# Scaled keys in eight tiles without a copy, weight maxima held to the end, and the staging of weights partly in x2T

## The chip, the cores and the metric

One core of one Trainium2 chip runs the whole program. The metric is device time in microseconds (us), the median of several runs; less is better.

## What is computed

The reference is a recurrent attention over 768 steps for 4 batches of 8 heads with a 40x40 state, followed by two dense layers on its 3072 rows of 320 values:

```
for t in range(S):
    y[:, :, t] = einsum('bhd,bhde->bhe', rt, state)
    Sa = einsum('bhde,bhe->bhd', state, at)
    state = state * wt[:, :, None, :] - outer(Sa, bt) + outer(vt, kt)
x = y as (3072, 320)
h = x @ w_in;  x = (h * cos(h)) @ w_out
h = x @ w_in2; out = (h * clip(h + 3, 0, 6) / 6) @ w_out2
```

The weights arrive as 64-bit floats.

## The kernel before

The 768 steps are cut into 12 chunks of 64. A unit n is one chunk of one batch, so there are 48. For a unit, `pA` loads r, k, a, b into `raw` and the running decay into `pip`; `pB` multiplies the two and splits the scaled keys into a high and a low half in `KBs` (L834 to L837) and the scaled queries likewise in `ARs`. `pT` transposes both by DMA to `KBT` and `ART`, and `pC` multiplies them on TensorE (tile `p`). `iB` inverts a triangular matrix for the four units of a chunk in 31 short steps on VectorE (tiles `tmp`, `Tt`, `Lt`). `cU`, `cA`, `cG` and `cF` compute the unit's output and the new state (tiles `u`, `FS`, `gm`, `GF`, `xy`, `S8a`, in PSUM mostly `t`). `cF` multiplies the keys in their natural layout once more. For that, `pB` copies the first 80 of every 128 columns of `KBs`, of which there are two tiles, into one of eight tiles `E` (L842, L843).

When the four units of a chunk are done, `mA` and `mB` run the first dense layer on its 256 rows (input `x1T`), and later the second (input `x2T`, which `mT` fills by DMA transposes). `mA` makes a PSUM tile `h`, ScalarE and VectorE make `s` from it and split it into two halves `ghl`, and `mB` adds the product with the weights up in `acc`. A layer of a chunk has 8 such groups. Below, a chunk's first multiplication means the first VectorE row that writes `s` from `h` in the first layer.

The weights come in 44 tiles of 128x512 values (22 for each layer). `ld_w` loads one to a staging place, `prep_w` turns it into a 32-bit value in a second staging place and splits it into two f16 halves in `win` and `wout`. The staging place is a piece of `wout` that is not filled yet or, for 16 tiles, `wstat` (`stage`, L735 to L748). `wmax` takes the largest absolute value of each finished tile on VectorE (a TENSOR_REDUCE into `acc` of the accumulators); the flags at the end of the program read it, and nothing before. A flag that fails starts a general path, which these data do not take.

The order of the instructions of each engine is not the order of the source. `Plan` records every operation with an estimated cost and its dependencies, goes forward and backward through a model of the engines `PASSES` times, and issues in the order of the last pass. An operation on `nc.either` goes to VectorE or GpSimd, or, for a copy, to VectorE or ScalarE, as the model finds it. So nearly every instruction carries the line of `emit` (L452, copies on ScalarE L448). All loads and transposes are issued by SyncE (SP).

Of the kernel before, what the change touches and what calls it, by code (L numbers as in the profile page):

```python
# [26 lines left out]
NT = B * S  # L27
HD = H * D
GRP = 4
NG = NC // GRP  # L30
SC = 256.0
ISC = 1.0 / 256.0
# [14 lines left out]

HALVES = ((0, 0), (1, 0))
SHARE = 20
SLACK, AHEAD, MARGIN = [0, 0, 0, 0, 0], [100, 100, 200, 0], [20, 20, 20, 0]  # L50
LAND = 1950
PASSES = 46
RING = {"raw": 2560, "KBT": 2048, "LN": 2048, "v": 1280, "uh": 640, "FT": 2048, "gm": 2048, "pd": 2560, "xy": 1280,
        "wst": 2048, "wx": 1024, "s": 2048, "xs2": 1536, "ghl": 2048, "E": 1280, "ART": 2048, "NT": 1152}


class Rings:
# [22 lines left out]
ALTS = {"ANY": ("DVE", "POOL"), "CPY": ("DVE", "ACT")}  # L80
T_SHAPE = 96.0
FULL = (128, 128)
POOL_GAIN = -0.03
OFFSET = 110
LAT = {"PE": 190, "DVE": 125, "ACT": 140, "POOL": 70}

# [1 line left out]
class Plan:  # L88
# [68 lines left out]
    def rec(self, attr, eng, name, a, kw):  # L157
# [25 lines left out]
        elif eng == "PE":  # L183
            m = _free(ins[0])
            c = max(n / 2.4 + 2.5, 25.0 if m == 128 else 32.0)
            if ins[0].dtype == F32:
                c = max(2 * (5 + 0.835 * m), 4 * n / 2.4)
            shape = tuple(32 if x <= 32 else 64 if x <= 64 else 128 for x in (ins[0].shape[0], _free(ins[0])))
        elif eng in ("DVE", "ANY"):
            c = 70 + n * 1.042  # L190
            es = max(mybir.dt.size(x.dtype) for x in outs + ins)
            if name == "tensor_copy":
                c = 70 + n * (0.26 if es == 2 else 0.52)
            elif name == "tensor_tensor" and n > 512 and any(len(x.ap) > 2 and abs(x.ap[-1][0]) > 4 for x in ins):
                c = 70 + n * 1.906
            elif name == "tensor_scalar":
                c = 70 + n * 0.52
            elif name == "reciprocal":
                c = 70 + n * 6.3
            elif name == "tensor_tensor_scan":  # L200
                c = 70 + n * 2.08
            if any(_free(x) == 1 for x in ins):
                c += 60
        elif eng == "ACT":
            c = 95 + n * 0.833
            if "accum_out" in kw:
                c += 93
            elif "bias" in kw:
                c += 50
            elif ins[0].tensor._space == PSUM:  # L210
                c -= 42
        rate = 2.56 if any(abs(x.ap[-1][0]) > 4 for x in ins) else 2.1 if all(mybir.dt.size(x.dtype) == 4 for x in outs + ins) else 1.88
        cp = 36 + n * 0.83 if name == "memset" else 150 + n * (rate if name == "tensor_tensor" else 3.4)
        if eng == "POOL":
            c = cp
        elif eng == "ANY" and name == "tensor_copy":
            eng, cp = "CPY", 95 + n * 0.833
        merge = eng == "PE" and self.ops and self.ops[-1]["eng"] == "PE" and self.ops[-1]["grp"] == (self.group, outs[0].tensor.name)
        if merge:
            i -= 1  # L220
# [121 lines left out]
    def forward(self, pr, pred, users):  # L342
# [41 lines left out]
        def arrive(u):  # L384
            e = ops[u]["eng"]
            ready_t[u] += SLACK[engs.index(e)] if e in engs else 0
            heapq.heappush(evs, (ready_t[u], 0, u))
            if e in engs[:4]:
                soon[engs.index(e)].add(u)
# [106 lines left out]
def kernel(  # L496
# [24 lines left out]
    p1 = Rings(big, 1)  # L521
    p2 = Rings(big, 2)
    p3 = Rings(big, 3)
    pE = Rings(big, 8)
    pA_ = Rings(big, 8)
    pN = Rings(big, 6)
    dr = pool("dr", 1, space=DRAM)
# [20 lines left out]
        COL[nm] = (ncol, ncol + k)  # L548
        ncol += k
    acc = fl.tile([128, ncol], F32, name="acc")  # L550
    KBss = [big.tile([128, H, 128], F16, name=f"KBs{i}") for i in range(2)]
    ARss = [big.tile([128, H, 128], F16, name=f"ARs{i}") for i in range(2)]
    pip0 = big.tile([128, H, 2, D], F32, name="pip0")
    TTp = big.tile([128, NH * C + 64], F16, name="TT")
# [169 lines left out]


    wflat = [t.rearrange("p x k f -> p x (k f)") for t in wout]
    wstat = big.tile([128, 1536], F32, name="wstat")
    junk = wstat[:, 1376:1536].bitcast(BF16)
    WST = {}

    def stage(m, kind, i):
# [4 lines left out]
        else:  # L736
            r, x = ((4, 8), (14, 18), (-1, 0), (4, 8), (14, 18), (-1, 0), (6, 18), (-1, 0), (-1, 0), (-1, 0))[i]
        if r < 0:
            return wstat[:, 0:1024], wstat[:, 1024:1536]
        w = wflat[m].rearrange("p x f -> p (x f)").bitcast(F32)  # L740
        return w[:, 256 * r:256 * r + 1024], w[:, 256 * x:256 * x + 512]

# [79 lines left out]
        ldq.dma_start(out=pip[0:64].rearrange("p h x e -> p h (x e)"), in_=dec(n).rearrange("h t x e -> t h (x e)"))  # L822
        st_raw[n] = (raw, pip)

    E_t = {}
    ART_t = {}
    KBT_t = {}

    def pB(n):
# [1 line left out]
        nc.either.tensor_copy(out=pip[64:128, :, 1], in_=pip[0:64, :, 1])  # L831
        rf = raw.rearrange("p h x e -> p (h x e)")
        nc.either.tensor_tensor(out=rf, in0=rf, in1=pip.rearrange("p h x e -> p (h x e)"), op=ALU.mult)
        kb, ar = KBss[n % 2], ARss[n % 2]  # L834
        kv = kb[:, :, 0:120].rearrange("p h (x e) -> p h x e", e=D)
        nc.either.tensor_copy(out=kv[:, :, 0::2, :], in_=bc2(raw[:, :, 1]))
        dp("kb", E_KB).tensor_tensor(out=kb[:, :, 40:80], in0=raw[:, :, 1], in1=kb[:, :, 0:40], op=ALU.subtract)  # L837
# [1 line left out]
        nc.either.tensor_copy(out=av, in_=bc2(raw[:, :, 0]))  # L839
        dp("ar", E_AR).tensor_tensor(out=ar[:, :, 80:120], in0=raw[:, :, 0], in1=ar[:, :, 0:40], op=ALU.subtract)  # L840
        square(rf, 0, 128, 640, "raw", n, rf)
        E_t[n] = pE.tile([128, H, 2 * D], F16, tag="E", name="E")  # L842
        nc.either.tensor_copy(out=E_t[n], in_=kb[:, :, 0:2 * D])  # L843
        later(0.7, pT, n)

    def pT(n):
        KBT_t[n] = p1.tile([128, H, 128], F16, tag="KBT", name="KBT")
        ART_t[n] = pA_.tile([128, H, 128], F16, tag="ART", name="ART")
        tq.dma_start_transpose(out=KBT_t[n], in_=KBss[n % 2].rearrange("p h e -> p (h e)"))
        tq.dma_start_transpose(out=ART_t[n], in_=ARss[n % 2].rearrange("p h e -> p (h e)"))  # L850

    NT_t = {}
# [188 lines left out]

    def cF(n):
        c, b = divmod(n, B)
        pd, kb, art = PD_t.pop(n), E_t.pop(n), ART_t.pop(n)
        gh, gl = ([t[:, h * (C + D):h * (C + D) + 128] for h in range(H)] for t in GFt)
        f = ps_t.tile([128, 512], F32, tag="t", name="gf")
        fv = f[:, 0:HD].rearrange("p (h e) -> p h e", h=H)
# [457 lines left out]
```

## Time and profile before

| | before |
|---|---|
| median of 3 runs | 1179.76 us (1177.58 to 1183.35) |
| the profiled execution | 1175.69 us |
| its span, first to last instruction | 1173.9 us |
| TensorE busy | 891.6 us, 76% |
| VectorE busy | 1009.4 us, 86% |
| ScalarE busy | 824.4 us, 70% |
| GpSimd busy | 200.8 us, 17% |
| mean granted TensorE clock | 0.966 |

Busy times are the time in which an engine has at least one instruction under way. In the trace PE is TensorE, PEld its weight loads, DVE VectorE, ACT ScalarE, POOL GpSimd, SP the queue of SyncE. Rows give a group of equal instructions as "out<-in", their number, the busy time and the mean time of one in ns, and then the idle time of the engine before them with what ended it.

### The profile page before, as it was taken

What the parts mean: (1) busy time and instruction counts of PE and PEld (TensorE: products, weight loads), DVE (VectorE), ACT (ScalarE), POOL (GpSimd) and SP (SyncE); (2) the same over time, 40 slices, a digit from 0 to 9 for tenths busy, and PEclk for the clock granted to TensorE, in tenths of its full rate; (3) what the DMA queues carried; (4) which work ended last, traced back from release to release, by engine and by line L of the source; (5) the groups of instructions that cost most, each with busy time, mean ns of one, the idle gap of its engine ahead of it and who ended that gap; (6) DMA issues with size and microseconds to landing.
All of it is one profiled execution on the core that took longest, in us unless ns stands there. A gap on an engine that the chain in (4) does not pass through costs nothing. (4 is left out here: it accounts for less than half of the span.)

```text
span 1173.9 us, 29549 instructions
## 1 busy us (share of the span) xinstructions
PE 891.6 (76%) x11378; PEld 727.0 (62%) x11378; DVE 1009.4 (86%) x2282; ACT 824.4 (70%) x1701; POOL 200.8 (17%) x225
## 2 busy tenths in 40 slices
PE   0010042265997999999999998999999999999994
PEld 0000031264775887787788777777778878788873
DVE  7799999979998999799998998988989879676552
ACT  5667688778988778688697876867758747563341
POOL 3340223433433102011020110300201000000000
PEclk9999999987998999899999999998999999999997
DMA  6988879978887677977778976797775773521010
GB/s 210 243 193 202 225 180 227 195 166 166 190 171 139 122 134 133 169 143 132 142 118 173 167 132 127 134 157 139 129 142 103 112 136 62 98 55 32 1 26 15
DMA packets 474361, 162.63 MB, mean 139 GB/s; under 512 B 446790, under 2 KB 456050, under 8 KB 473827
## 3 DMA queue, kind: packets, MB, share of 16 engines
q1 hardware_dynamic: 473922, 159.99, 68.8%
q8 instruction: 91, 1.49, 0.6%
q10 hardware_dynamic: 288, 0.67, 0.2%
q14 instruction: 60, 0.48, 0.1%
HBM read 80.09 MB, written 25.61 MB: 90 GB/s over the span
## 5 line engine op out<-in xcount | busy, mean ns | idle before, releaser
L452 PE MATMUL acc<-wout,ghl 128*128 128x320 f16 x2304 | 361.0, 304 | 11.7 <-DVE xs L452 6.8
L452 PEld LDWEIGHTS <-win 128*128 128x128 f16 x3328 | 309.6, 101 | 55.4 <-issue 14.8
L452 PEld LDWEIGHTS <-ghl 128*128 128x128 f16 x2304 | 218.3, 99 | 92.5 <-issue 7.7
L452 ACT ACTIVATE s<-h,cvec 128x512 f32<-128x512 f32 x192 | 130.5, 680 | 120.5 <-PE h L452 70.7
L452 PE MATMUL h<-x1T,win 128*128 128x256 f16 (+1 forms) x1664 | 194.1, 276 | 10.8 <-DVE s L452 10.4
L452 PE MATMUL h<-x2T,win 128*128 128x256 f16 (+1 forms) x1664 | 184.4, 266 | 2.5 <-DVE s L452 2.5
L452 DVE TENSOR_TENSOR ghl<-s,ghl 128x512 f16<-128x512 f32 x185 | 128.2, 693 | 5.0 <-ACT ghl L448 2.6
L452 PE MATMUL p<-ART,KBT 120*128 120x64 f16 x384 | 21.9, 206 | 143.7 <-DMA ART<-ARs 90.9
L452 PEld LDWEIGHTS <-KBT 120*128 120x128 f16 x384 | 18.5, 106 | 147.6 <-DMA KBT<-KBs 110.4
L452 DVE TENSOR_TENSOR tmp<-Tt,Lt 128x126 f32<-128x126 f32 (+22 forms) x372 | 103.3, 278 | 7.7 <-DMA Lt<-Ls 4.1
L452 DVE TENSOR_TENSOR Tt<-Tt,tmp 128x126 f32<-128x126 f32 (+22 forms) x372 | 105.2, 283 | 3.9
L452 DVE SCALAR_TENSOR_TENSOR s<-h,s 128x512 f32<-128x512 f32 x96 | 65.6, 686 | 39.1 <-ACT s L452 38.3
L448 ACT ACTIVATE ghl<-s 128x512 f16<-128x512 f32 x121 | 75.4, 625 | 26.2 <-DVE s L452 21.7
L452 DVE SCALAR_TENSOR_TENSOR s<-s,h 128x512 f32<-128x512 f32 x96 | 65.1, 680 | 23.6 <-ACT s L452 23.4
L452 POOL TENSOR_TENSOR wout<-wout 128x512 int32<-128x512 int32 (+2 forms) x30 | 47.9, 1600 | 102.6 <-ACT wout L452 46.0
L452 PE MATMUL t<-E,GF 128*128 128x40 f16 x1152 | 45.4, 183 | 23.0 <-DVE GF L452 18.1
L452 PEld LDWEIGHTS <-GF 128*128 128x128 f16 x1152 | 38.3, 98 | 30.5 <-DVE GF L452 18.8
L452 PE MATMUL t<-FS,NT 128*128 128x40 f16 x768 | 36.6, 182 | 20.4 <-DVE FS L452 13.6
L452 PEld LDWEIGHTS <-ART 120*64 120x64 f16 (+1 forms) x704 | 43.1, 105 | 14.3 <-issue 10.6
L452 PE MATMUL q<-Lt,Tt 32*32 32x32 f32 x768 | 31.6, 199 | 23.4 <-DMA Lt<-Tm 22.5
L452 ACT ACTIVATE wout<-wout 128x512 f32<-128x512 f32 (+3 forms) x56 | 37.0, 662 | 15.6 <-DMA wout<-in_moe_w_in_dram 11.3
L452 POOL TENSOR_TENSOR wstat<-wstat 128x512 int32<-128x512 int32 (+1 forms) x16 | 30.4, 1898 | 102.5 <-ACT wstat L452 80.4
(163 smaller groups left out, 1744.7 us busy)
## 6 DMA issues: line engine op xcount, KB each, us to landing
raw<-in_arbk_dram SPq DMA_DIRECT2D x46, 320.0 KB
v<-in_vv_dram SPq DMA_DIRECT2D x96, 80.0 KB
pip<-Dec SPq DMA_DIRECT2D x46, 160.0 KB
wout<-in_moe_w_in_dram SPq DMA_DIRECT2D x12, 512.0 KB
Ls<-LN SPq DMA_DIRECT2D x48, 128.0 KB
Lt<-Ls SPq DMA_DIRECT2D x48, 128.0 KB
TT<-Thl SPq DMA_DIRECT2D x12, 512.0 KB
wstat<-in_moe_w_out_dram SPq DMA_DIRECT2D x10, 512.0 KB
```

What stands on the lines that cost most here:

```text
L448: self.nc.scalar.activation(func=AF.Copy, **kw)
L452: getattr(getattr(self.nc, attr), name)(*a, **kw)
```

## The change

`KBs` has eight tiles instead of two, `cF` reads them directly, and the tiles `E` and their 48 copies are gone. The operations of `wmax` are held in the planner's model until 900000 of its units. `wstat` has 1024 columns instead of 1536; the second staging place of the 16 tiles that are staged there is now a part of `x2T`, and the scratch output `junk` lies in the last 160 columns of what is left. The planner's numbers are others: its slack, look-ahead and margins, its number of passes, the gain from which it gives GpSimd an operation, and the cost of a cast of a strided output. Six more small memsets on GpSimd clear the ends of the new tiles.

```diff
+NKB = 8
-SLACK, AHEAD, MARGIN = [0, 0, 0, 0, 0], [100, 100, 200, 0], [20, 20, 20, 0]
+SLACK, AHEAD, MARGIN = [0, 49, 4, 0, 67], [50, 50, 0, 0], [0, 100, 50, 0]
-PASSES = 46
+HELD, HOLD = ("wmax",), 900000
+PASSES = 29
-POOL_GAIN = -0.03
+POOL_GAIN = 0.17
...
+        turn = name == "tensor_copy" and n > 512 and abs(outs[0].ap[-1][0]) > 4
+        if turn:
+            c = 70 + n * 1.906
...
-            eng, cp = "CPY", 95 + n * 0.833
+            eng, cp = "CPY", 70 + n * 1.906 if turn else 95 + n * 0.833
...
             ready_t[u] += SLACK[engs.index(e)] if e in engs else 0
+            if ops[u]["grp"][0][0] in HELD:
+                ready_t[u] = max(ready_t[u], HOLD)
...
-    KBss = [big.tile([128, H, 128], F16, name=f"KBs{i}") for i in range(2)]
+    KBss = [big.tile([128, H, 128], F16, name=f"KBs{i}") for i in range(NKB)]
...
-    wstat = big.tile([128, 1536], F32, name="wstat")
-    junk = wstat[:, 1376:1536].bitcast(BF16)
+    wstat = big.tile([128, 1024], F32, name="wstat")
+    junk = wstat[:, 864:1024].bitcast(BF16)
...
-            return wstat[:, 0:1024], wstat[:, 1024:1536]
+            return wstat, x2T.rearrange("p a b -> p (a b)").bitcast(F32)[:, 0:512]
...
-        kb, ar = KBss[n % 2], ARss[n % 2]
+        kb, ar = KBss[n % NKB], ARss[n % 2]
...
-        E_t[n] = pE.tile([128, H, 2 * D], F16, tag="E", name="E")
-        nc.either.tensor_copy(out=E_t[n], in_=kb[:, :, 0:2 * D])
...
-        tq.dma_start_transpose(out=KBT_t[n], in_=KBss[n % 2].rearrange("p h e -> p (h e)"))
+        tq.dma_start_transpose(out=KBT_t[n], in_=KBss[n % NKB].rearrange("p h e -> p (h e)"))
...
-        pd, kb, art = PD_t.pop(n), E_t.pop(n), ART_t.pop(n)
+        pd, kb, art = PD_t.pop(n), KBss[n % NKB], ART_t.pop(n)
```

How the order moves is seen at three places. The first is VectorE near the start of the program, while the first weights are split (`win_68` is the first layer's, `wout_70` its still empty second matrix that serves as staging, `FS` the first unit's values). Before:

```order
L452 SCALAR_TENSOR_TENSOR FS_82<-v_136,FS_82 128x8x40
L452 TENSOR_REDUCE acc<-win_68 128x1
L452 TENSOR_TENSOR win_68<-wout_70,win_68 128x512
L452 CAST win_68<-wstat 128x512
L452 TENSOR_REDUCE acc<-win_68 128x1
L452 TENSOR_TENSOR win_68<-wstat,win_68 128x512
L452 TENSOR_REDUCE acc<-win_68 128x1
```

and now:

```order
L460 TENSOR_TENSOR win_68<-wout_70,win_68 128x512
L460 SCALAR_TENSOR_TENSOR FS_88<-v_134,FS_88 128x8x40
L460 CAST win_68<-wout_70 64x512
L460 TENSOR_TENSOR win_68<-wout_70,win_68 64x512
L460 TENSOR_SCALAR wout_70<-wout_70 128x512
L460 SCALAR_TENSOR_TENSOR wout_70<-wout_70 128x512
L460 TENSOR_TENSOR win_68<-x2T,win_68 128x512
```

The maxima are gone from here; up to the first chunk's first multiplication VectorE has 441 instructions before and 403 now, with 28 maxima before and none now.

The second is VectorE in the last sixth of the program, where the first layer of the eleventh chunk runs (`s_145`, `s_146`) beside the last chunk's attention. Before:

```order
L452 SCALAR_TENSOR_TENSOR s_147<-h_145,s_147 128x512
L452 CAST ghl_150<-s_147 128x512
L452 TENSOR_TENSOR ghl_150<-s_147,ghl_150 128x512
L452 SCALAR_TENSOR_TENSOR s_148<-h_146,s_148 128x512
L452 CAST ghl_151<-s_148 128x512
L452 TENSOR_TENSOR ghl_151<-s_148,ghl_151 128x512
L452 SCALAR_TENSOR_TENSOR s_147<-h_145,s_147 128x512
```

and now:

```order
L460 SCALAR_TENSOR_TENSOR s_145<-h_143,s_145 128x512
L460 TENSOR_REDUCE acc<-wout_70 128x1 x7
L460 SCALAR_TENSOR_TENSOR s_145<-h_143,s_145 128x512
L460 TENSOR_REDUCE acc<-wout_70 128x1
L460 SCALAR_TENSOR_TENSOR s_146<-h_144,s_146 128x512
L460 TENSOR_REDUCE acc<-wout_70 128x1
L460 TENSOR_REDUCE acc<-win_69 128x1 x2
```

All 44 maxima now stand between the last multiplication of the tenth chunk's first layer and the first one of the last chunk's, 8 of them ahead of the eleventh chunk's first multiplication, and the subtractions into `ghl` that stood there go to GpSimd (7 in the program before, 17 now).

The third is SP, where the first chunk's `x2T` is filled (`xs`) for the second layer and the last weights of that layer are loaded to `wstat`. Before:

```order
L452 DMA_TRANSPOSE x2T<-xs_153 128x6x128
L452 DMA_TRANSPOSE FT_141<-FS_82 128x8x128
L452 DMA raw_116<-in_arbk_dram 128x640
L452 DMA_TRANSPOSE ST_87<-Tt 128x16x48
L452 DMA_TRANSPOSE KBT_125<-KBs_76 128x8x128
L452 DMA Srep_89<-Tt 40x16x40 x3
L452 DMA Tt<-Ls_104 32x32x32
L452 DMA_TRANSPOSE FT_141<-FS_83 128x8x128
L452 DMA wstat<-in_moe_w_out_dram 128x1024
L452 DMA pip_80<-Dec_99 64x8x80
L452 DMA_TRANSPOSE x2T<-xs_154 128x6x128
```

and now:

```order
L460 DMA wstat<-in_moe_w_out_dram 128x1024
L460 DMA_TRANSPOSE ST_93<-Tt 128x16x48
L460 DMA Srep_95<-Tt 40x16x40 x2
L460 DMA_TRANSPOSE FT_139<-FS_88 128x8x128
L460 DMA Srep_95<-Tt 40x16x40
L460 DMA Tt<-Ls_110 32x32x32
L460 DMA_TRANSPOSE x2T<-xs_151 128x6x128
L460 DMA_TRANSPOSE FT_139<-FS_89 128x8x128
L460 DMA v_134<-in_vv_dram 64x320 x2
L460 DMA_TRANSPOSE x2T<-xs_152 128x6x128
```

Before, two loads to `wstat` follow the first transpose into `x2T` (one stands here, one seven rows later); now every load to `wstat` precedes it.

## Rows read from the trace of the kernel before

**Rows 1.** The page's busy times: us, share of the span, instructions.

```profile
PE 891.6 (76%) x11378; PEld 727.0 (62%) x11378; DVE 1009.4 (86%) x2282; ACT 824.4 (70%) x1701; POOL 200.8 (17%) x225
```

**Rows 2.** Busy time of each engine in five stretches; columns as the first line says.

```profile
core 0: us, PE busy (x) PEld busy (x) DVE busy (x) ACT busy (x) POOL busy (x), PEclk, DMA share, GB/s
0.00:241.60 241.60, 38.17 (x688) 33.45 (x688) 219.25 (x423) 172.99 (x332) 69.73 (x78) 1.00 0.87 207
241.60:398.50 156.90, 122.04 (x1681) 100.34 (x1682) 144.50 (x316) 133.84 (x285) 58.81 (x50) 0.87 0.79 162
398.50:1002.00 603.50, 577.99 (x7394) 469.67 (x7392) 550.45 (x1349) 449.14 (x943) 72.28 (x98) 0.98 0.75 134
1002.00:1151.50 149.50, 147.50 (x1578) 119.70 (x1576) 91.08 (x184) 66.00 (x140) 0.00 (x0) 1.00 0.20 38
```

**Rows 3.** The same view for the whole start and for the stretch 960 to 1036.

```profile
0.00:398.50 398.50, 160.22 (x2368) 133.80 (x2369) 363.75 (x738) 306.82 (x617) 128.54 (x127) 0.95 0.84 190
960.00:1036.00 76.00, 73.47 (x940) 60.22 (x937) 61.44 (x161) 46.55 (x101) 2.59 (x3) 1.00 0.42 72
```

**Rows 4.** What writes the accumulators on VectorE: number, ns min/median/max, first and last start.

```profile
L452 DVE TENSOR_REDUCE acc<-win x24: 664/674/686, 31.4 to 295.9; 128x1 f32<-128x512 f16 x16, 64x1 f32<-64x512 f16 x8
...
L452 DVE TENSOR_REDUCE acc<-wout x20: 666/673/686, 129.4 to 391.7; 128x1 f32<-128x512 f16 x20
```

**Rows 5.** Groups by cost: the copies to E.

```profile
L448 ACT ACTIVATE E<-KBs 128x640 f16<-128x640 f16 x46 | 33.4, 727 | 0.8 <-PE t L452 0.4
...
L452 DVE COPY E<-KBs 128x640 f16<-128x640 f16 x2 | 0.7, 325 | 0.0
```

**Rows 6.** Groups on VectorE by form, of the kinds whose number changes most.

```profile
L452 DVE TENSOR_TENSOR ghl<-s,ghl 128x512 f16<-128x512 f32 x185 | 128.2, 693 | 5.0 <-ACT ghl L448 2.6
...
L452 DVE CAST ghl<-s 128x512 f16<-128x512 f32 x71 | 30.8, 433 | 6.4 <-PE acc L452 4.2 <-DVE s L452 0.5
...
L452 DVE TENSOR_TENSOR KBs<-raw,KBs 128x320 f16<-128x320 f32 x39 | 20.0, 512 | 1.3 <-ACT KBs L448 1.1
L452 DVE TENSOR_TENSOR ARs<-raw,ARs 128x320 f16<-128x320 f32 x37 | 18.5, 500 | 0.3 <-ACT ARs L448 0.2
...
L452 DVE CAST KBs<-raw 128x640 f16<-128x640 f32 x10 | 6.9, 690 | 0.1
...
L452 DVE COPY GF<-FS 128x320 f16<-128x320 f16 x28 | 6.6, 234 | 0.1
...
L452 DVE TENSOR_TENSOR wout<-wout 128x512 f16<-128x512 f32 x8 | 5.4, 680 | 0.0
...
L452 DVE CAST Tt<-S8a 40x640 f16<-40x640 f32 x6 | 2.9, 490 | 2.2 <-DMA Srep<-Tt 2.1
```

**Rows 7.** Waits on VectorE: us in total, times, longest.

```profile
DVE s L452 <- ACT s L452: 61.6, 51, 4.1
```

**Rows 8.** What touches KBT: the transposes, ns min/median/max.

```profile
L452 SPq DMA_TRANSPOSE KBT<-KBs x48: 1231/1272/2387, 49.2 to 945.6; - x48
```

**Rows 9.** VectorE in order of time near 28 us: start, duration.

```profile
27.98 1.51 DVE L452 TENSOR_SCALAR wout<-wout 64x512 int32<-64x512 int32 x1
...
31.42 0.69 DVE L452 TENSOR_REDUCE acc<-win 128x1 f32<-128x512 f16 x1 [0.81 <-ACT win L448]
```

**Rows 10.** GpSimd in order of time in the same stretch.

```profile
27.53 1.68 POOL L452 TENSOR_TENSOR wout<-wout 128x512 int32<-128x512 int32 x1 [18.08 <-DVE wstat L452]
30.40 1.36 POOL L452 TENSOR_TENSOR wstat<-wstat 128x512 int32<-128x512 int32 x1 [1.19 <-ACT wstat L452]
```

**Rows 11.** SP in order of time: the two transposes that fill x2T first.

```profile
330.41 1.26 SPq L452 DMA_TRANSPOSE x2T<-xs  x1
...
344.68 1.29 SPq L452 DMA_TRANSPOSE x2T<-xs  x1
```

**Rows 12.** TensorE in order of time: the second layer's first matmuls.

```profile
351.26 1.95 PE L452 MATMUL h<-x2T,win 128*128 128x128 f16 x32
```

**Rows 13.** VectorE in order of time: the last read of wstat by the weights.

```profile
385.46 1.35 DVE L452 TENSOR_TENSOR wout<-wstat,wout 128x512 f16<-128x512 f32 x1
```

More of the change, by code (lines that the diff above doesn't have):

```diff
@@ L49 @@
 SHARE = 20
-SLACK, AHEAD, MARGIN = [0, 0, 0, 0, 0], [100, 100, 200, 0], [20, 20, 20, 0]
+SLACK, AHEAD, MARGIN = [0, 49, 4, 0, 67], [50, 50, 0, 0], [0, 100, 50, 0]
 LAND = 1950
-PASSES = 46
+HELD, HOLD = ("wmax",), 900000
+PASSES = 29
 RING = {"raw": 2560, "KBT": 2048, "LN": 2048, "v": 1280, "uh": 640, "FT": 2048, "gm": 2048, "pd": 2560, "xy": 1280,
-        "wst": 2048, "wx": 1024, "s": 2048, "xs2": 1536, "ghl": 2048, "E": 1280, "ART": 2048, "NT": 1152}
+        "wst": 2048, "wx": 1024, "s": 2048, "xs2": 1536, "ghl": 2048, "ART": 2048, "NT": 1152}
 class Rings:
@@ L523 @@
     p3 = Rings(big, 3)
-    pE = Rings(big, 8)
     pA_ = Rings(big, 8)
@@ L823, in pA @@
         st_raw[n] = (raw, pip)
-    E_t = {}
     ART_t = {}
```

## The prediction

> **What bounds the kernel now.** I read the page's busy times first, then the busy times by stretch, because an average over this program hides that its stages have different limits. TensorE is busy for 891.6 of 1173.9 us [rows 1]. Cut at the first dense matmul (241.6 us), at the first layer of the third chunk (398.5) and at that of the eleventh (1002), the stretches show two limits [rows 2]. Up to 241.6 us TensorE works 38.17 us while VectorE is busy for 219.25, or 91%; up to 398.5 us VectorE is still at 144.50 of 156.90, or 92%. After that TensorE has little idle time left: 25.5 us of 603.5 (603.50 less 577.99), then 2.0 us of 149.5. VectorE is close behind it in the long middle, 550.45 of 603.50, and free in the last stretch, 91.08 of 149.50.
>
> So the end is TensorE's work plus its idle time, and 238 us of that idle time lie ahead of 398.5 us (203.4 and 34.9), where VectorE sets the pace. Work that leaves VectorE there brings the rest forward; work that comes to VectorE behind 1002 us costs only where the gaps there do not take it. All 44 maxima start between 31.4 and 391.7 us [rows 4], in the stage where VectorE is dearest.
>
> **The change part by part.** The sum is made against the profiled execution, 1175.69 us; the median of the runs is 4.1 us above it, and I add the sum to the median. About 0.5% (5.9 us) is what a measurement of this kernel can tell from no change.
>
> *Maxima out of the start.* 36 of the 44 now stand behind the eleventh chunk's first multiplication: 36 x 0.674 = 24.3 us less on VectorE ahead of it [rows 4].
>
> *What the planner puts in their place.* The order has, up to the same point, 10 more casts into KBs (0.690 us each), 9 more copies into GF (0.234), 7 and 3 more subtractions into ARs and KBs (0.500, 0.512) and 10 more subtractions of weights (0.680): 6.9 + 2.1 + 5.0 + 6.8 = 20.8 us. It has 6 fewer casts into Tt (0.490), and 2 fewer subtractions and 2 fewer casts into ghl (0.693, 0.433): 5.2 us [rows 6]. The kinds left out are small and go both ways. Net, VectorE is relieved by 24.3 - 20.8 + 5.2 = 8.7 us. I count this in full, since VectorE is at 91 to 92% in every stretch ahead of 1002 us [rows 2]. The bounds are 0, if TensorE's queue is the limit in the middle, and 24.3, if the work put in falls where VectorE had room.
>
> *Copies to E.* 46 run on ScalarE for 33.4 us, two on VectorE for 0.7 [rows 5]. ScalarE is busy for 824.4 us [rows 1], so 4.1% of its work goes. VectorE waits 61.6 us for ScalarE's s [rows 7]; 4.1% of that is 2.5 us, which I take. Bounds: 0, because ScalarE is not the fullest engine anywhere, and 25.5, since what it gives the middle cannot exceed TensorE's idle time there [rows 2]; 2.5 is nearer to the row of the waits.
>
> *A wait in the place of the copy.* The write of KBs for unit n now waits for the state update of unit n-8, as the copy to E did; behind it stand the unit's low half, its transpose and the product p, and on ScalarE the next s. The copies to E had an idle time of 0.8 us before them in all [rows 5], so I take 0. The other end: cast, low half and transpose, 0.690 + 0.512 + 1.272 = 2.5 us [rows 6, 8], late once for each of ten chunks, 25 us. The queue of TensorE holds dense groups beside p, so 0 is nearer. The transposes of ART had to wait for the same update before.
>
> *Maxima at the end.* The remaining 36 bring 24.3 us to VectorE, and 8 subtractions into ghl leave it for GpSimd there (8 x 0.693 = 5.5): 18.8 us net. They stand where the eleventh chunk's first layer runs, in the trace of before about 960 to 1036 us; there VectorE has 76.00 - 61.44 = 14.6 us free [rows 3]. So 4.2 us do not fit. TensorE is full there and does not feel every delay of VectorE; I take half, 2.1 us. Bounds 0 and 18.8.
>
> *Staging in x2T.* The first transposes into x2T must now follow the last read of a staged weight. In the order that read stands 47 rows of VectorE ahead of the second layer's first multiplication, so I take 0; the other end is a rival below. The six memsets and the move of junk fall into idle time of GpSimd (69.73 us busy of 241.60) and of ScalarE's scratch: 0 [rows 2].
>
> Sum: -8.7 - 2.5 + 2.1 = -9.1 us. That is 1179.76 - 9.1 = **1170.7 us**, or 1166.6 for an execution like the profiled one.
>
> *What GpSimd takes from it.* At 27.98 us a TENSOR_SCALAR of VectorE on 64x512 takes 1.51 us while GpSimd has an operation under way, and at 31.42 us a maximum beside a GpSimd operation takes its usual 0.69 [rows 9, 10]. The Trainium skill (SBUF — State Buffer, section Who interferes with whom) says that VectorE and GpSimd share one pair of ports as an exclusive lock, and that tensor_reduce never contends for it here, while casts in a two-port mode and operations with two inputs in SBUF do. These rows agree with it. By that rule the maxima were the right filler beside GpSimd, and what fills their place waits; the sum by it is the first rival.
>
> **The rivals.**
> *Relief given back beside GpSimd.* GpSimd is busy for 128.54 of the first 398.50 us, 32% [rows 3]. If a maximum that ran beside it was free, and its successor there waits, 0.32 x 44 x 0.674 = 9.6 us are given back: 1179.76 - 9.1 + 9.6 = 1180.3 us, no change. For it: the 1.51 us above. Against it: GpSimd's mean share is spread unevenly, and it gets no more work there now. Chance 0.20.
>
> *The start counts, the filling does not.* VectorE loses 28 maxima ahead of the first dense multiplication, 18.9 us, and has 441 instructions before it then and 403 now. If TensorE's dense work begins that much sooner and the later additions find room, the gain is 18.9 + 2.5 = 21.4: 1158.4 us. Against it: VectorE has only 53 us free in the 603.50 of the middle [rows 2]. Chance 0.20.
>
> *The second layer starts late (slower).* In the trace of before x2T is filled first at 330.41 and 344.68 us [rows 11], the second layer's first matmul starts at 351.26 [rows 12], and the last subtraction that reads a staged weight at 385.46, for 1.35 us [rows 13]. With the new staging the fill must follow that subtraction: 385.46 + 1.35 + 6.6 (351.26 less 344.68) = 393.4 us, 42.1 later than now. VectorE's 44 maxima all lie ahead of it and bring it forward by 29.7, so 12.4 us remain as idle time of TensorE, the relief is used up there, and 12.4 - 2.5 + 2.1 = +12.0: 1191.8 us. It decides as soon as the weights are not finished 41 us sooner than now. For it: DMA is at 0.87 and 0.79 there [rows 2], so loads cannot come much sooner. Against it: the order puts all loads to wstat ahead of the fill and other loads behind it. Chance 0.15.
>
> **How the numbers follow.** The forecast has 0.45. Faster by over 0.5% (below 1173.9 us) is the forecast and the early start: 0.65. Within 0.5% is the relief given back: 0.20. Slower by over 0.5% is the late second layer: 0.15. The range reaches down past the early start to the point where the whole 24.3 us of the maxima and the 2.5 count (1179.76 - 26.8 = 1153), and up to just below the late second layer: **1153 to 1190 us**. It leaves out the late second layer in its full size and part of the upper bounds of the wait on KBs.
>
> **What would show it.** In the changed kernel's profile there should be no copy to E and no maximum before about 900 us; the first dense matmul some 15 to 20 us ahead of 241.6; the second layer's first matmul at 335 to 350 instead of 351.26; the third chunk's first layer 5 to 10 us ahead of 398.5 us, and the eleventh's about 10 us ahead of 1002. ScalarE's busy time should fall to about 785 us and VectorE's should be higher by some us. The prediction is wrong if the second layer's first matmul comes after 355 us, if TensorE's idle time between the third and the eleventh chunk grows over the 25.5 us of now because KBs copies wait for the state update, or if the last chunk's first layer waits behind the maxima.

## Result: slower by about 1%

The changed kernel takes 1189.72 us (median of 12 runs, 1184.87 to 1197.71), the kernel before beside it 1177.68 (12 runs, 1172.56 to 1183.35). The ratio is 1.0095, with a 95% interval of [1.0072, 1.0118]: some 11 us slower, where I forecast 9 us faster. The profiled execution took 1192.52 us with a span of 1190.1.

The busy times of the page, to set beside [rows 1]:

```profile
PE 898.3 (75%) x11378; PEld 727.7 (61%) x11378; DVE 1016.1 (85%) x2301; ACT 790.8 (66%) x1643; POOL 191.1 (16%) x222
```

ScalarE lost 33.6 us, the size of the copies to E, and stands near the forecast of 785; VectorE gained 6.7. Next the stretches of [rows 2], cut at the same events of the changed kernel: the first dense matmul (234.3 us), the first layer of the third chunk (393.2) and of the eleventh (1019.6), and the last layer's end. The columns are those of the first line.

```profile
core 0: us, PE busy (x) PEld busy (x) DVE busy (x) ACT busy (x) POOL busy (x), PEclk, DMA share, GB/s
0.00:234.30 234.30, 30.35 (x552) 26.46 (x552) 208.30 (x401) 167.25 (x323) 67.54 (x75) 1.00 0.86 211
234.30:393.20 158.90, 126.07 (x1856) 104.21 (x1853) 149.44 (x344) 125.94 (x266) 39.17 (x39) 0.88 0.82 164
393.20:1019.60 626.40, 585.89 (x7339) 471.69 (x7340) 547.32 (x1325) 429.30 (x909) 73.24 (x99) 0.96 0.71 129
1019.60:1170.20 150.60, 150.00 (x1595) 121.28 (x1594) 107.05 (x225) 66.77 (x142) 11.13 (x10) 1.00 0.20 38
```

The start is ahead: the first dense matmul by 7.3 us, the third chunk by 5.3. The last stretch is as long as before (150.6 against 149.5) though the maxima now stand at its head. The whole loss is in the middle, 626.4 us against 603.5, +22.9. VectorE works a little less there (547.32 against 550.45) and ScalarE 20 us less; TensorE's idle time grows from 25.5 to 40.5 us (626.40 less 585.89), and its work stretches by 7.9 us at a lower granted clock (0.96 against 0.98). So VectorE and ScalarE have less to do in the middle, and TensorE's work is the same but runs slower; for the rest the engines wait more.

Up to the eleventh chunk's first layer VectorE is busy for 208.30 + 149.44 + 547.32 = 905.1 us, against 914.2 before. That is a relief of 9.1 us where the sum had 8.7. But its idle time up to there rose from 1002 - 914.2 = 87.8 us to 1019.6 - 905.1 = 114.5. The relief was there, and 26.7 us of idle time swallowed it.

Who is waited for in the middle is spread thin. Lines of the waits between 393 and 1020 us (engine and what it writes, what it waits for: us in all, times, longest):

```profile
DVE s L460 <- ACT s L460: 33.5, 26, 5.1
...
PE q L460 <- DMA Lt<-Tm: 14.1, 6, 4.2
...
ACT KBs L456 <- PE t L460: 3.8, 5, 1.4
...
PE p L460 <- DMA KBT<-KBs: 3.3, 3, 1.6
```

And before, between 398 and 1002 us, where no copy into KBs waited for TensorE:

```profile
DVE s L452 <- ACT s L452: 16.5, 17, 3.0
...
PE q L452 <- DMA Lt<-Tm: 4.1, 3, 2.0
...
PE p L452 <- DMA KBT<-KBs: 3.3, 3, 1.6
```

The line ACT KBs is the wait that I had priced at nothing. By itself it is 3.8 us. TensorE's own wait for the transposed keys did not grow, 3.3 us in both. Its wait in front of q did; these are products at the end of the inversion, which starts from the p of a chunk's four units. What the wait on KBs does to the order is seen on one unit, the first of the tenth chunk. In the changed kernel (start, duration, engine, what; put together from the views in order of time of TensorE, SP and VectorE):

```profile
747.33 0.57 PE L460 MATMUL t<-KBs,GF 128*128 128x40 f16 x16
747.42 1.23 SPq L460 DMA_TRANSPOSE ART<-ARs  x1
748.12 0.47 DVE L460 CAST KBs<-raw 128x640 f16<-128x640 f32 x1
749.55 1.23 SPq L460 DMA_TRANSPOSE KBT<-KBs  x1
773.19 0.39 PE L460 MATMUL p<-ART,KBT 120*128 120x64 f16 x8
```

And the same unit in the kernel before, from the same views and ScalarE's:

```profile
695.08 0.72 ACT L448 ACTIVATE KBs<-raw 128x640 f16<-128x640 f32 x1
715.92 1.28 SPq L452 DMA_TRANSPOSE KBT<-KBs  x1
734.33 0.57 PE L452 MATMUL t<-E,GF 128*128 128x40 f16 x16
735.50 1.26 SPq L452 DMA_TRANSPOSE ART<-ARs  x1
739.27 0.72 ACT L448 ACTIVATE E<-KBs 128x640 f16<-128x640 f16 x1
748.90 0.40 PE L452 MATMUL p<-ART,KBT 120*128 120x64 f16 x8
```

The line with t is the end of the state update (the products of `cF`) eight units back. Before, the cast and the transpose of the keys were done 39 and 18 us ahead of it. The copy to E had to stand behind it, and so had the transpose of the queries into ART, which p needs as well. Now the cast comes 0.2 us after its end, and transpose and p after the cast. Counted over units 8 to 47 in the two traces: before, 37 of the 40 casts start ahead of the end of that update, and the median of all 40 is 18.3 us ahead; after, none does, and 21 of 40 start within 2 us of it. The planner has packed the keys against their new limit. The keys' transpose starts 1.4 us ahead of that end in the median before and 7.3 us behind it after; it is later than the queries' in 17 units before and in 32 after. p itself starts 11.0 us behind that end in the median before and 16.0 after.

The maxima moved as said, beside [rows 4]: number, ns min/median/max, first and last start.

```profile
L460 DVE TENSOR_REDUCE acc<-win x24: 666/670/685, 987.1 to 1048.8; 128x1 f32<-128x512 f16 x16, 64x1 f32<-64x512 f16 x8
L460 DVE TENSOR_REDUCE acc<-wout x20: 666/668/686, 1031.3 to 1060.4; 128x1 f32<-128x512 f16 x20
```

And the second layer, beside [rows 11, 12]: the weights' last read of x2T on VectorE, the first transposes into x2T on SP, the first matmul on TensorE.

```profile
338.30 0.69 DVE L460 TENSOR_TENSOR wout<-x2T,wout 128x512 f16<-128x512 f32 x1
```

```profile
339.02 1.25 SPq L460 DMA_TRANSPOSE x2T<-xs  x1
...
344.35 2.12 SPq L460 DMA_TRANSPOSE x2T<-xs  x1
```

```profile
350.88 1.95 PE L460 MATMUL h<-x2T,win 128*128 128x128 f16 x32
```

The first transpose starts 0.03 us after the weights' read has ended. The second layer begins where it did before (351.26).

### The profile page after: what moved, and what is told of

Its sections match the earlier page's. It is cut to its first block, busy times and chain, and to the rows that moved or that the text cites. A ratio compares the mean times of both kernels' runs of the same rounds, so it can differ in the third digit from the quotient of the medians.

```text
span 1190.1 us, 29506 instructions
## 1 busy us (share of the span) xinstructions
PE 898.3 (75%) x11378; PEld 727.7 (61%) x11378; DVE 1016.1 (85%) x2301; ACT 790.8 (66%) x1643; POOL 191.1 (16%) x222
## 5 line engine op out<-in xcount | busy, mean ns | idle before, releaser
L460 PE MATMUL acc<-wout,ghl 128*128 128x320 f16 x2304 | 367.3, 305 | 7.5 <-DVE ghl L460 6.0
L460 PE MATMUL h<-x1T,win 128*128 128x256 f16 (+1 forms) x1664 | 197.0, 278 | 5.4 <-DVE s L460 4.9
L460 DVE TENSOR_TENSOR ghl<-s,ghl 128x512 f16<-128x512 f32 x175 | 120.4, 688 | 4.4 <-ACT ghl L456 2.0
L460 DVE TENSOR_TENSOR tmp<-Tt,Lt 128x126 f32<-128x126 f32 (+22 forms) x372 | 107.1, 288 | 7.0 <-POOL Tt L460 1.9
L460 DVE TENSOR_TENSOR Tt<-Tt,tmp 128x126 f32<-128x126 f32 (+22 forms) x372 | 98.7, 265 | 4.2
L456 ACT ACTIVATE ghl<-s 128x512 f16<-128x512 f32 x124 | 77.4, 625 | 33.6 <-DVE s L460 26.7
L460 POOL TENSOR_TENSOR wout<-wout 128x512 int32<-128x512 int32 (+1 forms) x28 | 50.4, 1802 | 124.2 <-ACT wout L460 78.0
L460 PE MATMUL t<-KBs,GF 128*128 128x40 f16 x1152 | 45.2, 183 | 31.9 <-DVE GF L460 31.1
L460 PEld LDWEIGHTS q<-Lt,Tt 32*32 32x32 f32 x768 | 29.7, 117 | 39.4 <-DMA Lt<-Tm 34.3
L460 PE MATMUL t<-FS,NT 128*128 128x40 f16 x768 | 36.6, 183 | 20.5 <-DVE FS L460 12.0
L460 POOL TENSOR_TENSOR S8a<-S8a,xy 40x320 f32<-40x320 f32 x18 | 21.9, 1217 | 150.4 <-DVE xy L460 147.5
```

Of the source, the lines that this page charges most:

```text
L456: self.nc.scalar.activation(func=AF.Copy, **kw)
L460: getattr(getattr(self.nc, attr), name)(*a, **kw)
```

## The experiments

Theories: **keys** (the wait in the place of the copy), **numbers** (the planner's SLACK, AHEAD, MARGIN and POOL_GAIN), **staging** (x2T), **held maxima**, and **any new order**: each edit makes the planner write another order of the instructions, and that alone may move the time. In every run PASSES was set anew; where two runs differ in PASSES alone, they are two orders of one program. Ratios are to runs of the kernel before on the same chip.

**The parts, one upon the other.** The held maxima alone:

```diff
-PASSES = 46
+PASSES = 13
+HELD, HOLD = ("wmax",), 900000
...
+            if ops[u]["grp"][0][0] in HELD:
+                ready_t[u] = max(ready_t[u], HOLD)
```

> The kernel before with one part of the change alone: the weight maxima are held back. Keys are still copied to E, staging and the planner's numbers are those of before. The start gained 7.3 us in the changed kernel. Theory 'keys' (the write of KBs waits for the state update eight units back, and costs the middle): that wait is not in this kernel, so the relief of the start comes through: 1170 to 1174 us against 1177.7, the first layer of the eleventh chunk 5 to 8 us ahead of 1002 us. Theory 'held maxima' (what fills their place, or the maxima at the end, costs more than they gave): 1184 to 1190 us, as after. Theory 'numbers' and theory 'staging': as 'keys', 1170 to 1174. Theory 'any new order' (the planner's order is another each time, and most are worse than the one before, whatever is changed): above 1182.

Measured: 1169.69 us, ratio 0.9887 [0.9852, 0.9921], as "keys" expected and a little more. This version beats both kernels. Its stretches, cut at the same events:

```profile
0.00:395.40 395.40, 160.87 (x2393) 136.07 (x2394) 358.63 (x738) 303.64 (x613) 102.98 (x106) 0.94 0.86 193
395.40:997.00 601.60, 574.66 (x7394) 466.79 (x7392) 546.84 (x1352) 451.56 (x937) 70.44 (x99) 0.98 0.74 134
997.00:1144.70 147.70, 146.84 (x1550) 118.64 (x1549) 100.73 (x197) 67.84 (x143) 10.40 (x9) 1.00 0.21 37
```

With the staging in x2T as well (the diff's three lines on wstat, junk and x2T; PASSES 46):

> As the run with the held maxima, and the staging partly in x2T as well. Keys are still copied to E, the planner's numbers are those of before. Theory 'keys' and theory 'numbers': no more than 2 us above the run with the held maxima, so 1170 to 1176 us. Theory 'staging' (the second layer's first fill of x2T must wait for the weights, and the loads of weights with it): 1182 to 1190 us, with the loss ahead of the third chunk. Theory 'any new order': above 1182 with the loss anywhere.

Measured: 1175.19 us, 0.9938 [0.9914, 0.9963]: inside the 1170 to 1176 of "keys" and "numbers", but 5.5 us above the run with the held maxima, where they allowed 2. In this run the second layer starts at 353 us, in the one ahead of it at 327.76:

```profile
327.76 1.96 PE L455 MATMUL h<-x2T,win 128*128 128x128 f16 x32
```

With the keys as well, so that only the planner's numbers are left out of the change (the planner's cost of turned copies, that is of casts of a strided output, which the diff also has, is in wherever there are key tiles; PASSES 24):

```diff
-SLACK, AHEAD, MARGIN = [0, 49, 4, 0, 67], [50, 50, 0, 0], [0, 100, 50, 0]
+SLACK, AHEAD, MARGIN = [0, 0, 0, 0, 0], [100, 100, 200, 0], [20, 20, 20, 0]
...
-POOL_GAIN = 0.17
+POOL_GAIN = -0.03
```

> The whole change except for the planner's numbers (SLACK, AHEAD, MARGIN and POOL_GAIN are those of before): it differs from the run with held maxima and staging in x2T by the keys in eight tiles alone. Theory 'keys': slower than that run by 10 to 20 us, TensorE's idle time between the third and the eleventh chunk 35 us or more (25.5 before, 40.5 after), and copies into KBs that wait for TensorE. Theory 'numbers': the same as that run within 3 us, TensorE's idle time there 20 to 27 us. Theory 'any new order': differs in either sign.

Measured: 1187.66 us, 1.0059 [1.0036, 1.0082]: 1.2% above the run without the keys, inside what "keys" expected. But TensorE's idle time in the middle is 39.5 us (623.60 less 584.14) where the run with copies had 36.6 already, and copies into KBs waited for the state update for 1.8 us in all, so the idle time of one profile does not carry the verdict:

```profile
390.60:1014.20 623.60, 584.14 (x7391) 471.88 (x7389) 552.82 (x1323) 430.69 (x911) 92.62 (x113) 0.97 0.71 130
```

The planner's numbers alone, put into the kernel before (PASSES 56):

> The kernel before with the planner's numbers of the change alone (SLACK, AHEAD, MARGIN, POOL_GAIN and the cost it gives to turned copies stay as stated there; keys copied to E, no held maxima, staging as before). Theory 'numbers' (they order the middle worse): 1185 to 1192 us, TensorE's idle time between the third and the eleventh chunk near 40 us. Theory 'keys' and theory 'staging': 1174 to 1182 us, as before. Theory 'any new order': above 1182.

Measured: 1204.66 us, 1.0179 [1.0142, 1.0217], the slowest of all and 12 us above what "numbers" expected; TensorE's idle time in the middle is 30.9 us there, not near 40. In the whole change, with the keys, the numbers add little (1.0095 against 1.0059).

**How far ahead the keys may be written.** Seven tiles (NKB = 7, PASSES 32):

> As the run with held maxima, staging in x2T and keys (1187.66 us), but with seven key tiles, so that the write of KBs for unit n waits for the state update of unit n-7. In the traces the cast into KBs of unit n stood 8 or 9 state updates ahead of the last finished one where keys were copied to E, and exactly 7 with eight key tiles, so at the limit each time. Theory 'keys, by their lead': it stands at 6 now and the time grows again by 10 to 20 us, to 1198 to 1208. Theory 'keys, by the shape read' or 'any new order' (what costs is not how far ahead KBs may be written): within 5 us of 1187.66.

Measured: 1192.91 us, 1.0067 [1.0042, 1.0091], the same as with eight. The expectation of "keys, by their lead" failed, but the run is not what it was meant to be: in the program the write of one unit in four is recorded ahead of the state update seven units back, so that for these units the update reads another unit's keys, and for these the wait is not there. So it decides nothing.

A ninth tile (PASSES 13):

```diff
+N9 = 20
...
+    KBss.append(wstat[:, 0:512].bitcast(F16).rearrange("p (h e) -> p h e", h=H))
...
+    def slot(n):
+        return n % NKB if n < N9 else (8, 4, 5, 6, 7, 0, 1, 2, 3)[(n - N9) % 9]
...
-        kb, ar = KBss[n % NKB], ARss[n % 2]
+        kb, ar = KBss[slot(n)], ARss[n % 2]
+        if n == N9:
+            nc.gpsimd.memset(kb[:, :, 120:128], 0.0)
...
```

> As the run with held maxima, staging in x2T and keys (1187.66 us), but with a ninth key tile from unit 20 on, which lies in wstat when no weight is staged there any more. Theory 'keys, by their lead': the casts into KBs stand 8 state updates ahead from the sixth chunk on, about half of what the copies allowed more, and the time falls by 4 to 8 us, to 1180 to 1184. Theory 'any new order' or 'keys, by the shape read': within 3 us of 1187.66.

Measured: 1179.12 us, 0.9960 [0.9932, 0.9987], 1.0% below the run with eight. Of the 40 casts 18 now stand ahead of the update eight units back. The ninth tile is written first at 404.1 us, behind the start of the third chunk. The middle:

```profile
383.60:1002.50 618.90, 578.51 (x7382) 469.63 (x7379) 545.06 (x1318) 444.68 (x929) 86.71 (x115) 0.97 0.76 133
```

Copies to E with seven tiles of E (one number changed in the second run; PASSES 36):

> As the run with held maxima and staging in x2T, keys copied to E (1175.19 us), but with seven tiles of E instead of eight: the copy to E of unit n waits for the state update of unit n-7, and the write of KBs, which has two tiles, for that of n-9. Theory 'keys, by their lead': the path to p is let on 8 updates ahead, still one more than with eight key tiles, so 1176 to 1181 us. Theory 'how long a key must be kept' (fewer tiles cost, of whatever kind): near 1187. Theory 'any new order': either way.

Measured: 1179.46 us, 0.9962 [0.9941, 0.9983], inside the expectation of "keys, by their lead". But the keys of some units are overwritten ahead of their state update here too, so that it supports little.

The third run in another order (PASSES 22 in place of 24):

> The same program as the run with held maxima, staging in x2T and keys (1187.66 us), with the order of two planner passes earlier (22 passes in place of 24), whose plan is about as long. It shows what another order of the same instructions is worth. Theory 'keys': within 3 us of 1187.66. Theory 'any new order': differs by 5 us or more.

Measured: 1194.05 us, 1.0083 [1.0054, 1.0113], 2.8 us more than the first order by the ratios; the intervals overlap.

**The same in the whole change.** Copies to E put back, all else as in the change (PASSES 48):

```diff
-NKB = 8
+NKB = 2
...
+    pE = Rings(big, 8)
...
+        E_t[n] = pE.tile([128, H, 2 * D], F16, tag="E", name="E")
+        nc.either.tensor_copy(out=E_t[n], in_=kb[:, :, 0:2 * D])
...
-        pd, kb, art = PD_t.pop(n), KBss[n % NKB], ART_t.pop(n)
+        pd, kb, art = PD_t.pop(n), E_t.pop(n), ART_t.pop(n)
```

> The whole change except for the keys: they are copied to E again, with two tiles of KBs; held maxima, staging in x2T and the change's planner numbers stay. Theory 'keys, by their lead': the changed kernel's 0.95% goes, and the time is 1174 to 1182 us with before at 1181. Theory 'numbers': 1186 to 1192, as the changed kernel, since the numbers are still there.

Measured: 1189.46 us, 1.0053 [1.0034, 1.0073]. The time lies where "numbers" had it, 0.4% below the change: under half of the loss goes with the keys here. The casts run ahead again (35 of 40 ahead of the update eight units back).

The whole change with the ninth tile (PASSES 24):

> The changed kernel, all of it, with a ninth key tile from unit 20 on in the idle part of wstat. Theory 'keys, by their lead': 6 to 12 us below the changed kernel, as the ninth tile gave with the planner's old numbers (0.996 of before against 1.0059), so a ratio of 0.998 to 1.004. Theory 'any new order' (the ninth tile's gain was a lucky order): within 3 us of the changed kernel, ratio 1.007 to 1.012.

Measured: 1190.25 us, 1.0056 [1.0032, 1.0080], 0.4% (4.6 us) below the change: between the two expectations.

The staging in x2T alone (PASSES 31):

> The kernel before with the staging in x2T alone; maxima where they were, keys copied to E, the planner's numbers of before. The run with held maxima lost 6 us when the staging was added to it. Theory 'staging': 3 to 8 us above before, ratio 1.002 to 1.007, and the second layer starts behind 351 us. Theory 'any new order': a ratio on either side, the second layer's start where it was.

Measured: 1194.74 us, 1.0112 [1.0080, 1.0144], above what "staging" expected; the second layer starts at 366.8 us. Against the other orders of the kernel before, further below, it is 0.3%.

The nine tiles of the sixth run in another order (PASSES 28):

> The run with nine key tiles (ratio 0.996) once more with another order, of a planner pass whose plan is about as long (28 passes in place of 13). Theory 'keys, by their lead': ratio 0.993 to 0.999. Theory 'any new order': the gain of the ninth tile does not come back, ratio 1.003 to 1.009, as with eight tiles (1.0059 and 1.0083 in two orders).

Measured: 1185.51 us, 1.0027 [1.0003, 1.0051]: just outside both. Two orders of one program are 0.67% apart, with intervals that do not meet.

**What another order is worth.** Since that size is that of the parts, the next runs change PASSES and nothing else.

> The kernel before, unchanged but for the planner pass whose order is taken (29 in place of 46; the two plans are about as long). Theory 'the parts cost': ratio 0.997 to 1.003. Theory 'any new order' (the order of before was a good one, and any other loses, whatever the change): 1.004 to 1.012, so that most of what the staging (1.0112) or the keys lost was no cost of theirs.

Measured: 1190.95 us, 1.0077 [1.0053, 1.0101]. The kernel before, with no part of the change in it, loses 0.8% by another order. Its stretches:

```profile
0.00:406.80 406.80, 162.37 (x2392) 137.10 (x2393) 371.46 (x752) 312.46 (x623) 124.04 (x129) 0.95 0.84 187
406.80:1013.90 607.10, 573.92 (x7371) 466.50 (x7369) 542.82 (x1336) 447.86 (x934) 67.08 (x92) 0.98 0.72 131
1013.90:1167.40 153.50, 149.86 (x1573) 121.06 (x1571) 92.69 (x188) 65.08 (x137) 0.93 (x1) 0.98 0.22 41
```

> The held maxima alone (ratio 0.9887) in another order, of pass 26 in place of 13. Theory 'the parts cost': 0.985 to 0.993, the gain stays. Theory 'any new order': it shrinks to 0.994 or more.

Measured: 1182.76 us, 1.0006 [0.9976, 1.0036]: the held maxima's gain against the kernel before is gone in this order, as "any new order" had it.

> The whole change in another order, of pass 55 in place of 29. Theory 'the parts cost': 1.006 to 1.013, as the change (1.0095). Theory 'any new order': anywhere from 1.000 to 1.020, and if it comes out below 1.002 the result itself was an accident of the order.

Measured: 1194.21 us, 1.0094 [1.0057, 1.0131]: the result stands in a second order.

> Held maxima and staging in x2T with keys copied to E (ratio 0.9938) in another order, of pass 44 in place of 46. Theory 'the parts cost': 0.990 to 0.998, still below eight key tiles in both orders (1.0059, 1.0083). Theory 'any new order': above 1.001, so that copies and keys cannot be told apart.

Measured: 1176.92 us, 0.9958 [0.9940, 0.9976]: below eight key tiles in both orders.

> The kernel before in a third order, of planner pass 45 in place of 46, with a plan about as long. Theory 'the order of before was a good one': ratio 1.004 to 1.010 again. Rival 'the second order was a bad one': 0.997 to 1.003.

Measured: 1191.15 us, 1.0088 [1.0059, 1.0118]: the order of before is a good one; two others lose 0.8 and 0.9%.

> The held maxima alone in a third order, of pass 19 in place of 13 (0.9887) and 26 (1.0006). Theory 'held maxima gain about 0.9% against the kernel before in the mean over orders': 0.988 to 1.000. Rival 'the first order was an accident': 1.002 to 1.008, as other orders of the kernel before.

Measured: 1187.62 us, 1.0042 [1.0015, 1.0069], inside what "the first order was an accident" expected and outside the gain. It is above the kernel before and below the two other orders of it.

**Together**, with every order that ran (the middle is the third chunk's first layer to the eleventh's, in the profiled execution; the last column is TensorE's wait in the middle for the end of the inversion, the row PE q for Lt):

| program | ratios, by order | mean | third chunk at, us | middle, us | wait of q, us |
|---|---|---|---|---|---|
| before | 1 (the one given), 1.0077, 1.0088 | 1.0055 | 398.5, 406.8, 405.2 | 603.5, 607.1, 607.1 | 4.1, 3.6, 2.4 |
| held maxima | 0.9887, 1.0006, 1.0042 | 0.9978 | 395.4, 393.2, 394.2 | 601.6, 613.7, 618.2 | 5.7, 8.4, 11.2 |
| and staging in x2T | 0.9938, 0.9958 | 0.9948 | 387.5, 393.0 | 618.8, 610.8 | 7.9, 5.3 |
| and eight key tiles | 1.0059, 1.0083 | 1.0071 | 390.6, 397.2 | 623.6, 622.6 | 10.6, 9.7 |
| the same with nine | 0.9960, 1.0027 | 0.9994 | 383.6, 393.2 | 618.9, 622.6 | 2.4, 4.9 |
| and the numbers (the change) | 1.0095, 1.0094 | 1.0095 | 393.2, 401.9 | 626.4, 622.0 | 14.1, 15.2 |
| the change with copies to E | 1.0053 | | 400.9 | 618.1 | 9.2 |
| the change with nine key tiles | 1.0056 | | 395.1 | 623.2 | 10.4 |

By these means the keys cost 1.2% (14 us) with the planner's old numbers, its cost of turned copies included, and, by one order, 0.4% (5 us) with the new; the ninth tile gives back 0.8% and 0.4%. In both settings each run with copies or nine tiles lies below each run with eight, though some intervals overlap (1.0027 [1.0003, 1.0051] and 1.0059 [1.0036, 1.0082]). The wait of q goes the same way in both settings, though the held maxima alone reach 11.2 us in their third order. The held maxima give 0.8%, or 0.6% without the first order of either program; the staging gives nothing measurable, the numbers 0.2%.

With the planner's old numbers most of the ninth tile's gain is not where the tile is. It is written first at 404.1, 412.2 and, in the change, 395.9 us. In the profiled executions there, nine tiles are 10.7 and 5.4 us faster than eight; 7.0 and 4.0 us of this lie ahead of the third chunk, and so ahead of that first write, where only the order of the instructions differs. The middle is shorter by 4.7 and 0.0 us and, in the change, by 3.2.

## Why the prediction was wrong

**The step that failed is "A wait in the place of the copy", which I took at 0.** The comparisons of versions put 5 to 14 us in its place, inside the bounds of 0 and 25 that I had kept; the 14 have the planner's cost of turned copies in them, and another order alone can do as much. The reasoning erred at one point. From the 0.8 us of idle time ahead of the copies to E [rows 5] I concluded that the state update was no limit for the keys. But the copy was never on the way to p. It could stand 6.9 us in the median behind the update while the cast stood 18.3 us ahead of it, and its short wait told of a place in the order that the planner was free to choose. The question to put to the trace was how far ahead of that update the cast itself stood. It was in the rows of time of the kernel before, and 37 of 40 casts would have had to move. I was right that the transposes into ART stood behind the same update before: p had that limit already, and what is new is that the keys now come later than the queries.

That the casts stand at their limit now is shown by the traces. That the time hangs on it is supported and not shown. For it: with eight tiles each run is slower than with copies or nine, in both settings, and TensorE waits longer for the inversion that p feeds. Against it: the two settings give 14 and 5 us, where one program in another order moves by up to 18; most of the ninth tile's gain lies ahead of its first use; and in the held maxima alone, in their first order the fastest version, p starts over 20 us behind the update in the median, against 16.0 in the change, so that a late p is not enough to make a version slow. The path from the late cast to TensorE's 15 us of idle time was not traced wait by wait: the waits in the middle are many and short.

**What the sum was made against was one good order.** I added terms to the time of the kernel before as if the planner would keep the quality of its order. Any edit here makes a new order, and two other orders of the unchanged kernel are 0.8 and 0.9% slower, 9 to 10 us: as much as my whole sum, with no term in it for this. Orders of one program are 0.01% to 1.55% apart. By the means of the table the 11.2 us of loss add up as +6.5 from the order given to the mean of the orders of before, -9.1 for the held maxima, -3.5 for the staging, +14.5 for the keys and +2.8 for the numbers. How the last two share their sum hangs on which is added first: by the copies put back into the change the keys are 5 of it.

*Maxima out of the start, and what the planner puts in their place* (-8.7): right in size as VectorE's work, 9.1 us in the change, and 914.2 - (358.63 + 546.84) = 8.7 in the held maxima alone. As time it holds only against like orders: 0.9978 against 1.0055, -9 us. That these means come so close to the sum is partly luck, since the orders of the held maxima alone lie 18 us apart. The start is shorter in every order, the third chunk beginning at 395.4, 393.2 and 394.2 us against 398.5, 406.8 and 405.2. "I count this in full" was the weak part: the middle of two of the three orders is 10 and 15 us longer than that of the order given.

*Copies to E* (-2.5): no sign of it. ScalarE lost the 33.6 us, and VectorE's wait for its s is 63.5 us where it was 61.6 [rows 7]; in the change's second order it is 51.7, and 51.7 with the copies put back.

*Maxima at the end* (+2.1): right to about 1 us. The last stretch is 1.1 us longer, and TensorE is busy for 150.00 of its 150.60 us.

*Staging in x2T* (0): right for the time, though not for the reason that I gave. The rival *the second layer starts late* was right on the mechanism: the weights' last read ends 0.03 us ahead of the first transpose, and with the staging the second layer starts 25 to 32 us later than with the held maxima alone (353.1 and 357.4 against 327.8, 327.5 and 325.0). It does not decide, because TensorE has other work then: the third chunk starts no later (387.5 and 393.0). Nor did the second layer start later than in the kernel before, because the weights' last read of the staging ended 47.8 us sooner than there (338.99 against 386.81 [rows 13]). The forecast of 335 to 350 us for that matmul missed by a little, 350.88.

*What GpSimd takes from it*: the means hide it. Those of what took the maxima's place on VectorE did not grow (groups by form, the last figure ahead of the idle time is the mean in ns, to set beside [rows 6]):

```profile
L460 DVE TENSOR_TENSOR ARs<-raw,ARs 128x320 f16<-128x320 f32 x43 | 21.2, 493 | 0.1
L460 DVE TENSOR_TENSOR KBs<-raw,KBs 128x320 f16<-128x320 f32 x42 | 20.8, 496 | 0.7 <-ACT KBs L456 0.6
...
L460 DVE CAST KBs<-raw 128x640 f16<-128x640 f32 x20 | 10.2, 511 | 0.5 <-PE t L460 0.5
```

Before, these took 500, 512 and 690 ns. But a few long instructions make these means, as ns min/median/max show, before and after (so 0.690 us was too much for a cast in the sum):

```profile
L452 DVE TENSOR_TENSOR KBs<-raw,KBs x39: 461/484/1145, 46.1 to 933.2; 128x320 f16<-128x320 f32 x39
L452 DVE CAST KBs<-raw x10: 483/488/1584, 62.6 to 858.2; 128x640 f16<-128x640 f32 x10
```

```profile
L460 DVE TENSOR_TENSOR KBs<-raw,KBs x42: 473/479/1152, 52.9 to 940.0; 128x320 f16<-128x320 f32 x42
...
L460 DVE CAST KBs<-raw x20: 474/484/757, 65.1 to 938.5; 128x640 f16<-128x640 f32 x20
```

In the trace of before a subtraction into KBs takes 483 ns in the mean with no GpSimd operation beside it and 607 with one beside it for over half of its time; one into NT, which also reads two tiles, takes 686 and 1164; a maximum of wout takes 673 in both cases. The Trainium skill (SBUF — State Buffer, section Who interferes with whom) has operations with two inputs in SBUF contend with GpSimd, and a tensor_reduce not; the trace agrees. An estimate of the cost, what VectorE's instructions beside GpSimd take above the median of their form without it, comes to 33.2 us up to the third chunk before and 37.0 after, and to 51.8 and 53.9 us in all. So the rival *relief given back beside GpSimd* is there, at 2 to 4 us and not 9.6.

*The start counts*: the first dense matmul is 7.3 us ahead, not 18.9, and nothing of it reaches the end.

Of the three signs named as a refutation one came: TensorE's idle time in the middle is 40.5 us, over the 25.5 named, with copies into KBs behind the state update. The second layer's first matmul came within 355 us, and TensorE did not wait in the last stretch. On the slower side I named the wrong rival: I gave the late second layer 0.15 and the wait on KBs only a place in the bounds, though it had the larger upper end, 25 us.

**Left open.** The planner's cost of turned copies was not tried alone; it is in all runs with key tiles, and in the change with copies to E. Why the numbers cost 1.8% in the kernel before and little beside the keys was not followed up. How much of the keys' cost a tenth tile would return was not tried. How much of the ninth tile's gain is the tile's, and how much the order's, stays open too.

## What to carry to other kernels

When a copy is removed and its reader takes the source itself, the wait moves from the copy to the writer of the source and to all behind it; look at how far the writer ran ahead of that point before, and at what else on its path already stands behind the same point, and not at the idle time in front of the copy. Where a scheduler writes the order anew for each edit, run a second and third order of the unchanged program first: an effect that is no larger than their spread belongs to no part until it has been seen in two orders. A relief in busy time of the fullest engine is only a gain if its idle time does not grow, so follow both.

## What the runs showed of the hardware

Of the 22.9 us lost in the middle, 7.9 are TensorE running slower, not waiting: its granted clock there is 0.96, before 0.98, for about as many matmuls (7339 and 7394 records). In the change's second order it is 2.5 (580.46 us busy, at 0.97). I had counted its waiting alone. And one does not tell the other. The middle of the change with copies, and of the change with nine key tiles:

```profile
400.90:1019.00 618.10, 574.09 (x7332) 464.88 (x7330) 545.94 (x1323) 446.08 (x934) 73.94 (x104) 0.98 0.72 129
```

```profile
395.10:1018.30 623.20, 588.34 (x7344) 474.42 (x7342) 546.08 (x1338) 432.05 (x912) 78.83 (x98) 0.95 0.71 130
```

The first has 44.0 us of idle time at 0.98, the second 34.9 at 0.95, and the one with less idle time is the longer. TensorE's idle time alone does not measure what an order costs; the length of the stretch does.
